# Attention and two expert layers on one core: the first expert product by Strassen's method, fused with the second

## The chip, the core and the metric

The program runs on one core of a Trainium2 chip, whose engines work side by side and wait for each other through semaphores: TensorE (PE; matmuls into PSUM, eight banks of 512 float32 columns by 128 partitions), VectorE (DVE), ScalarE (ACT), GpSimd (POOL) and SyncE (SP), which issues the transfers. The metric is device microseconds of one execution. Three runs of the kernel before took 662.17 to 663.9 us, median 663.18.

## The reference

```python
attn = softmax(mask(q @ k.T / 8)) @ v        # 2 x 8 heads, 576 tokens, 64 wide; local or strided mask
x = attn as (1152, 512)
a = x @ w1;  b = x @ w2                      # (1152, 1024)
x = (a * b @ w3) @ w_out                     # (1152, 512)
p = domain_probs / (domain_probs.sum(-1, keepdims=True) + 1e-09)
for e in range(4):                           # moe2: w1 (4, 512, 1024), w2 (4, 1024, 512)
    h = np.maximum(x @ w1[e], 0.0)
    out += p[:, e:e + 1] * (h @ w2[e])
```

All of it is float32.

## The kernel before

A float32 operand is split into a high part in the reduced format fp32r (a ScalarE cast) and a low part, the rest (a VectorE subtraction). `mm3` (L244) makes a product of two such pairs from three matmuls: high by high, high by low, low by high.

The stages follow each other: attention in 22 tiles; the product a * b (`ab_block`), whose beginning runs beside the attention; w3 @ w_out (`wc_tile`); x3 = ab @ wc (`x3_block`, 16 blocks of 128 features by 288 tokens, 24 matmuls each); then the expert stage, four times over:

- first product (`g1_block`): 8 feature tiles by 3 blocks of 384 tokens. A block is 12 matmuls (4 tiles of 128 inputs, three matmuls each) into one PSUM bank; ScalarE writes relu of it as h_hi (L418), VectorE the rest as h_lo (L419). h for all 1152 tokens stays in SBUF.
- second product (`g2_tile`): 9 tiles of 128 tokens. A tile is 24 matmuls of 512 columns; VectorE scales the result by the token's probability and adds it to the sum (L445, L447). Of the last expert's last tile two halves of 256 columns are made. Finished sums go out at once (L450).

Expert weights come in chunks of 1 MB (`raw_load`), two buffers deep; a chunk is cast and subtracted a piece at a time (`split_hi` L152, `split_lo` L162) by a generator `work()`, which the main loop pushes on by `advance(n)` after each block. A count `live` of the 16 unit buffers (128 x 1024) holds it back. The order of instructions on each engine is that in which this Python code emits them; nothing is reordered. SP issues loads in the order of emission too, each held until its buffer is free.

Of the kernel before, what the change touches and what calls it, by code (L numbers as in the profile page):

```python
# [8 lines left out]
F32 = mybir.dt.float32  # L9
# [31 lines left out]
def kernel(  # L41
# [17 lines left out]
    big = ctx.enter_context(tc.tile_pool(name="big", bufs=16))  # L59
# [5 lines left out]
    small = ctx.enter_context(tc.tile_pool(name="small", bufs=4))  # L65
    ps = ctx.enter_context(tc.tile_pool(name="ps", bufs=5, space=bass.MemoryType.PSUM))
# [41 lines left out]
    class Chunk:  # L108


        def __init__(self, src, wide):
            self.src, self.wide, self.done, self.early = src, wide, False, False

        def raw_load(self):
            if self.wide:
                self.raw = rawp.tile([P, 1024, 2], I32, tag="raw", name="raw64")
                nc.sync.dma_start(out=flat(self.raw), in_=self.src.bitcast(I32))
            else:
                self.raw = rawp.tile([P, 2, 1024], F32, tag="raw", name="raw32")
                nc.sync.dma_start(out=self.raw, in_=self.src.rearrange("c p n -> p c n"))  # L120
# [51 lines left out]
    c_w12 = [Chunk(w12[c], True) for c in range(8)]  # L172
    c_wout = [Chunk(w_out[c], True) for c in range(4)]
    c_w3 = [Chunk(w3T[c], True) for c in range(8)]
    c_e = [Chunk(e12[2 * c:2 * c + 2], False) for c in range(4 * E)]
    live = 8
    stream = c_w12 + c_wout + c_w3 + c_e
    chunk32 = [Chunk(None, False) for _ in range(8 * E)]
# [9 lines left out]
    def work():  # L188


        wide = [c for c in stream if c.wide]
# [30 lines left out]
        for i, c in enumerate(chunk32):  # L222
            pair = c_e[i // 2]
            while live > 14:
                yield False
            c.f32 = pair.raw[:, i % 2]
            c.split_hi()
            yield True
            c.split_lo()
            if i % 2:  # L230
                load_next()
            yield True
# [7 lines left out]
    def need(c):  # L240
        while not c.done:
            assert advance()
# [12 lines left out]
    def load_group(b, g, zeros, cut=0):  # L255


        tq = [big.tile([P, 2, S], F32, tag="big", name="tq") for _ in range(2)]
        tk = big.tile([P, 2, S], F32, tag="big", name="tk")
# [107 lines left out]
    def ab_block(b, ft, n):  # L367
        t = slice(b * S + n * HB, b * S + n * HB + HB)
        if n == 0 and ft % 2 == 0:
            ab_hi[b, ft // 2] = big.tile([P, 2, S], F32R, tag="big", name="ab_hi")  # L370
            ab_lo[b, ft // 2] = big.tile([P, 2, S], F32R, tag="big", name="ab_lo")
# [24 lines left out]
    def x3_block(x3, wc, b, n, ot):  # L396
# [5 lines left out]
        hi, lo = (x[:, ot, t] for x in x3)  # L402
        nc.scalar.copy(hi, acc)
        nc.vector.tensor_tensor(out=lo, in0=acc, in1=hi.bitcast(F32), op=ALU.subtract)


    h_hi, h_lo = {}, {}

    def g1_block(e, x3, ft, n):
        t = slice(n * BLK, n * BLK + BLK)  # L410
        if n == 0:
            h_hi[ft] = big.tile([P, NT], F32R, tag="big", name="h_hi")
            h_lo[ft] = big.tile([P, NT], F32R, tag="big", name="h_lo")
# [4 lines left out]
        nc.scalar.activation(h_hi[ft][:, t], acc, AF.Relu)  # L418
        nc.vector.scalar_tensor_tensor(out=h_lo[ft][:, t], in0=acc, scalar=0.0,  # L419
                                       in1=h_hi[ft][:, t].bitcast(F32), op0=ALU.max, op1=ALU.subtract)  # L420

    pn = const.tile([P, NTT, E], F32, name="pn")
    sums = []
# [9 lines left out]
    def g2_tile(e, tt):  # L433
        t = slice(tt * P, tt * P + P)
        if e == 0 and tt % 2 == 0:
            sums.append(unit("sum", F32))
        total = sums[tt // 2][:, 512 * (tt % 2):512 * (tt % 2) + 512]
        width = 256 if (e, tt) == (E - 1, NTT - 1) else 512
        for c in (slice(c, c + width) for c in range(0, 512, width)):
            acc = bank("g2_acc")[:, c]  # L440
            for k in range(8):
                mm3(acc, (h_hi[k][:, t], h_lo[k][:, t]),
                    chunk32[8 * e + 4 + k // 2].parts(512 * (k % 2) + c.start, width), k == 0, k == 7)
            if e == 0:
                nc.vector.tensor_scalar_mul(total[:, c], acc, pn[:, tt, e:e + 1])  # L445
            else:
                nc.vector.scalar_tensor_tensor(out=total[:, c], in0=acc, scalar=pn[:, tt, e:e + 1],  # L447
                                               in1=total[:, c], op0=ALU.mult, op1=ALU.add)
            if e == E - 1:
                nc.sync.dma_start(out=out[t, c], in_=total[:, c])  # L450

    with tc.manual_schedule():
# [9 lines left out]
        for _ in range(2):  # L462
            pair = big.tile([P, 2, 4, P], F32, tag="big", name="p_pair")
# [55 lines left out]
        wc = [Chunk(None, False) for _ in range(4)]  # L519
# [18 lines left out]
        x3 = (xp.tile([P, 4, NT], F32R, tag="x_hi", name="x3_hi"), xp.tile([P, 4, NT], F32R, tag="x_lo", name="x3_lo"))  # L538
        for b in range(B):
            for i in range(2):  # L540
                for ot in range(4):
                    x3_block(x3, wc, b, i, ot)
                    advance(1)
        for c in wc[:3]:
            c.free()
        live += (NTT + 1) // 2
        for e in range(E):
            for ft in range(8):
                c = chunk32[8 * e + ft // 2]
                need(c)  # L550
                for i in range(NBLK):
                    g1_block(e, x3, ft, i)
                    advance(1)
                if ft % 2:
                    c.free()
            last = chunk32[8 * e + 4:8 * e + 8]
            for c in last:
                need(c)
            for tt in range(NTT):
                g2_tile(e, tt)  # L560
                if tt == NTT - 1:
                    for c in last:
                        c.free()
                advance(2)
# [62 lines left out]
```

## Time and profile before

| | us |
|---|---|
| median of three runs | 663.18 |
| profiled execution, its own time | 663.13 |
| its span, first to last instruction | 661.4 |
| TensorE busy | 647.7 |
| VectorE busy | 305.6 |
| ScalarE busy | 222.5 |

The span is what the engines' records cover; 1.7 us of the execution lie around it. Matmul records overlap, as matmuls are pipelined, so their mean duration is not what one costs; the distance between the ends of equal groups is. The expert stage fills the last 396 us.

### The profile page before, as it was taken

The numbers are of one execution on the slowest core, as the hardware profiler recorded it, in microseconds if no ns is written. First come the engines' busy times: TensorE is split into PE (matmuls) and PEld (weight loads), VectorE is DVE, ScalarE is ACT, GpSimd is POOL, SyncE is SP. The second block draws the span as 40 slices with busy tenths as digits, with TensorE's granted clock in tenths as the row PEclk, the third lists the DMA queues.
The fourth block names the chain that finished last, engine by engine and source line by source line (L and its number), as shares of the span: only waits on it lengthen the run. The fifth ranks groups of instructions, "written<-read, shape, count | busy, mean of one in ns | idle before, by whom it ended". The sixth has DMA issues, their size and how long they took to land.

```text
span 661.4 us, 9113 instructions
## 1 busy us (share of the span) xinstructions
PE 647.7 (98%) x3860; PEld 596.5 (90%) x3860; DVE 305.6 (46%) x514; ACT 222.5 (34%) x502; POOL 6.9 (1%) x18
## 2 busy tenths in 40 slices
PE   8879999999999999999999999999999999999998
PEld 7669989999888999999888999888999888999887
DVE  7999998699775411333212533212533212533111
ACT  5887776466654211223000423000423000422000
POOL 4000000000000000000000000000000000000000
PEclk9989999999999999999999999999999999999999
DMA  8933134154441300011000312000311000300111
GB/s 248 297 108 129 65 128 137 57 172 148 154 165 63 128 1 1 1 65 64 0 1 0 128 64 64 0 1 0 127 64 63 1 1 4 125 1 0 49 48 48
DMA packets 12809, 48.31 MB, mean 73 GB/s; under 512 B 1248, under 2 KB 2528, under 8 KB 10208
## 3 DMA queue, kind: packets, MB, share of 16 engines
q1 hardware_dynamic: 12624, 47.63, 21.9%
q8 instruction: 30, 0.49, 0.3%
q10 hardware_dynamic: 144, 0.10, 0.1%
q14 instruction: 11, 0.09, 0.0%
HBM read 45.37 MB, written 2.36 MB: 72 GB/s over the span
## 4 chain that ended last, share of the span: by engine, by line
PE 91%; DVE 7%; DMA 1%; ACT 0%; issue 0%; SPq 0%
PE g_acc L247 20%; PE g_acc L246 20%; PE g_acc L248 20%; PE ab_acc L246 5%; PE ab_acc L248 5%; PE ab_acc L247 5%; PE x_acc L246 3%; PE x_acc L247 3%; PE x_acc L248 3%; PE wc_acc L248 2%; PE wc_acc L246 2%; PE wc_acc L247 2%; DVE p_pair L326 1%; DVE neg L308 1%; PE sc L302 1%; PE o L345 1%
## 5 line engine op out<-in xcount | busy, mean ns | idle before, releaser
L418 ACT ACTIVATE h_hi<-g_acc 128x384 fp32r<-128x384 f32 x96 | 47.2, 492 | 274.3 <-PE g_acc L248 274.3
L248 PE MATMUL g_acc<-x_hi,w_lo 128*128 128x384 f32 x384 | 128.3, 334 | 0.0
L246 PE MATMUL g_acc<-x_hi,w_hi 128*128 128x384 f32 x384 | 128.3, 334 | 0.0
L247 PE MATMUL g_acc<-x_lo,w_hi 128*128 128x384 f32 x384 | 128.3, 334 | 0.0
L248 PE MATMUL g_acc<-w_hi,h_lo 128*128 128x512 f32 (+1 forms) x296 | 113.5, 384 | 0.0
L247 PE MATMUL g_acc<-w_lo,h_hi 128*128 128x512 f32 (+1 forms) x296 | 113.5, 384 | 0.0
L246 PE MATMUL g_acc<-w_hi,h_hi 128*128 128x512 f32 (+1 forms) x296 | 113.4, 383 | 0.0
L419 DVE SCALAR_TENSOR_TENSOR h_lo<-g_acc,h_hi 128x384 fp32r<-128x384 f32 x96 | 53.5, 558 | 120.2 <-ACT h_hi L418 120.2
L447 DVE SCALAR_TENSOR_TENSOR sum<-g_acc,pn,sum 128x512 f32<-128x512 f32 (+1 forms) x28 | 20.5, 732 | 123.3 <-PE g_acc L248 123.3
L246 PE MATMUL ab_acc<-x_hi,w_hi 128*128 128x288 f32 x256 | 76.5, 299 | 0.0
L248 PE MATMUL ab_acc<-x_hi,w_lo 128*128 128x288 f32 x256 | 75.4, 295 | 0.0
L247 PE MATMUL ab_acc<-x_lo,w_hi 128*128 128x288 f32 x256 | 75.4, 294 | 0.0
L246 PEld LDWEIGHTS g_acc<-x_hi,w_hi 128*128 128x128 f32 x384 | 72.1, 188 | 0.1
L247 PEld LDWEIGHTS g_acc<-x_lo,w_hi 128*128 128x128 f32 x384 | 72.1, 188 | 0.1
L248 PEld LDWEIGHTS g_acc<-x_hi,w_lo 128*128 128x128 f32 x384 | 72.1, 188 | 0.0
L246 PEld LDWEIGHTS g_acc<-w_hi,h_hi 128*128 128x128 f32 x296 | 55.6, 188 | 10.9
L248 PEld LDWEIGHTS g_acc<-w_hi,h_lo 128*128 128x128 f32 x296 | 55.6, 188 | 10.9
L247 PEld LDWEIGHTS g_acc<-w_lo,h_hi 128*128 128x128 f32 x296 | 55.6, 188 | 10.8
L246 PEld LDWEIGHTS ab_acc<-x_hi,w_hi 128*128 128x128 f32 x256 | 48.0, 187 | 1.5 <-issue 0.3
L247 PEld LDWEIGHTS ab_acc<-x_lo,w_hi 128*128 128x128 f32 x256 | 48.0, 188 | 0.0
L248 PEld LDWEIGHTS ab_acc<-x_hi,w_lo 128*128 128x128 f32 x256 | 48.0, 188 | 0.0
L162 DVE TENSOR_TENSOR w_lo<-raw,w_hi 128x1024 fp32r<-128x1024 f32 x32 | 38.8, 1216 | 0.3 <-ACT w_hi L152 0.3
(85 smaller groups left out, 835.8 us busy)
## 6 DMA issues: line engine op xcount, KB each, us to landing
raw<-in_e_dram SPq DMA_DIRECT2D x16, 1024.0 KB, 4.8
raw<-in_w_dram SPq DMA_DIRECT2D x8, 1024.0 KB, 5.0
raw<-in_w3T_dram SPq DMA_DIRECT2D x8, 1024.0 KB, 4.8
raw<-in_w_out_dram SPq DMA_DIRECT2D x4, 1024.0 KB, 4.9
out_dram<-sum SPq DMA_DIRECT2D x8, 256.0 KB, 2.0
tk<-in_kT_dram SPq DMA_DIRECT2D x3, 576.0 KB, 15.8
tq<-in_qT_dram SPq DMA_DIRECT2D x6, 288.0 KB, 13.7
tv<-in_v_loc_dram SPq DMA_DIRECT2D x4, 384.0 KB, 9.9
```

The costliest lines, as they stand in the source:

```text
L162: nc.vector.tensor_tensor(out=self.lo, in0=self.f32, in1=self.hi.bitcast(F32), op=ALU.subtract)
L246: mm(acc, lh, rh, start=first, stop=False)
L247: mm(acc, lh, rl, start=False, stop=False)
L248: mm(acc, ll, rh, start=False, stop=last)
L302: mm(self.sc[:nq, h, :nk], tq[h % 2][:, h // 2, self.q0:self.q0 + nq], tk[:, h // 2, self.k0:self.k0 + nk], start=False, stop=h == 3)
L308: nc.vector.tensor_reduce(out=self.neg[:nq], in_=self.sc[:nq, :, :nk], axis=mybir.AxisListType.X, op=ALU.max, negate=True)
L326: nc.vector.tensor_tensor(out=p, in0=p, in1=rec[:nq].unsqueeze(2).to_broadcast([nq, 4, nk]), op=ALU.mult)
L345: mm(self.o[64 * j:64 * j + 64, k, :nq], vs[k][:nk, self.t, 64 * j:64 * j + 64], self.pT[:nk, 2 * k + j, :nq], start=True, stop=True)
L418: nc.scalar.activation(h_hi[ft][:, t], acc, AF.Relu)
L419: nc.vector.scalar_tensor_tensor(out=h_lo[ft][:, t], in0=acc, scalar=0.0, in1=h_hi[ft][:, t].bitcast(F32), op0=ALU.max, op1=ALU.subtract)
L447: nc.vector.scalar_tensor_tensor(out=total[:, c], in0=acc, scalar=pn[:, tt, e:e + 1], in1=total[:, c], op0=ALU.mult, op1=ALU.add)
```

## The change

Tokens are cut into two halves, of five tiles (640) and four (512), and the whole expert stage runs for the one half and then for the other. A step is one half, one expert and one chunk c of 256 features: 2 x 4 x 4 = 32 steps, 0 to 15 and 16 to 31. In a step the inputs (512) by features (256) matrix of weights and the inputs by tokens matrix are cut in quarters, and h of the step is made of seven products of quarters (`Step.first`) and sums of them; each product has 6 matmuls of 320 or 256 columns. Three PSUM banks a, b, c take the products in turn: a, b, c, a, b, c, a. VectorE adds them into u1, u2, u3, u7 in SBUF (u1 begins as a ScalarE copy), from where ScalarE makes relu (h_hi) and VectorE h_lo. The second product of a step (`Step.second`, 6 matmuls a tile) is interleaved with the first product of the next step: three tiles at the `yield`s of `first`, the others behind it. Its sums stay open in one PSUM bank a tile over the four chunks of an expert, so `g2_acc` holds five banks.

The sums of quarters on the tokens' side are made once for each half (`Tokens.prepare`, eleven pieces): for the first half during the last x3 blocks, for the second in steps 14 and 15. Those on the weights' side are made in the first half (`Weights.work`), written to DRAM as cast pairs, and read back in the second half (`again`); the plain quarters and w2 are loaded and cast twice. x3 is kept as float32.

```diff
-    def g1_block(e, x3, ft, n):
...
-        acc = bank("g1_acc")[:, :BLK]
-        for k in range(4):
-            mm3(acc, chunk32[8 * e + ft // 2].parts(((ft % 2) * 4 + k) * P, P),
-                (x3[0][:, k, t], x3[1][:, k, t]), k == 0, k == 3)
...
+        def work(self):
+            nonlocal live
+            while live > 12:
+                yield False
+            live += 4
+            w = self.raw[:, 0]
...
+            yield from self.split([u[:, :768] for u in plain], w[:, 256:])
...
+            if not self.again:
+                add(a22, a21, a22, ALU.add)
+                add(a21, a11, a21, ALU.subtract)
+                yield True
+                add(a11, a22, a11, ALU.subtract)
+                add(a12, a12, a11, ALU.subtract)
+                yield True
+            sums = [unit("s_hi"), unit("s_lo")]
+            if self.again:
+                for i, u in enumerate(sums):
+                    nc.sync.dma_start(out=u.bitcast(F32), in_=stored[self.at][i])
+            else:
+                yield from self.split(sums, w)
+                for i, u in enumerate(sums):
+                    nc.sync.dma_start(out=stored[self.at][i], in_=u.bitcast(F32))
...
+            self.w2 = [unit("w2_hi"), unit("w2_lo")]
+            yield from self.split(self.w2, self.raw[:, 1])
+            self.done2 = True
+            load_next()
...
+            self.product(a, "a11", "b11")
+            nc.scalar.copy(u1, a)
+            self.product(b, "s2", "t2")
+            self.add(u2, b, u1)
+            work(1)
+            self.product(c, "s3", "t3")
+            self.add(u3, c, u2)
+            work(1)
+            self.product(a, "a12", "b21")
+            self.add(u1, a, u1)
+            self.out(0, 0, u1, 0)
+            yield
+            work(1)
+            self.product(b, "s1", "t1")
+            self.add(u7, b, u3)
+            self.out(1, 1, u7, 0)
+            self.add(u2, b, u2)
+            self.out(0, 0, u1, 1)
+            self.product(c, "a22", "t4")
+            self.add(u3, c, u3)
+            self.out(1, 0, u3, 0)
+            yield
+            self.out(1, 1, u7, 1)
+            work(1)
+            self.product(a, "s4", "b22")
+            self.add(u2, a, u2)
+            self.out(0, 1, u2, 0)
+            self.out(1, 0, u3, 1)
+            yield
+            work(1)
+            self.out(0, 1, u2, 1)
...
+            for i, _ in enumerate(step.first(advance)):
+                tile_of_tokens()
+                if s == 14:
+                    prepare(3, 7)
+            live -= 4
+            for _ in range(3):
+                tile_of_tokens()
```

Where instructions stand now, at three places. First VectorE in an expert's first product. Before, its rows behind those of x3 are the low parts of h (g_acc is the PSUM bank, h_lo the low part), with a low part of weights let in after several blocks:

```order
L404 TENSOR_TENSOR x_lo<-x_acc,x_hi 128x288 x11
L419 SCALAR_TENSOR_TENSOR h_lo<-g_acc,h_hi 128x384 x8
L162 TENSOR_TENSOR w_lo<-raw_2427,w_hi 128x1024
L419 SCALAR_TENSOR_TENSOR h_lo<-g_acc,h_hi 128x384 x6
L162 TENSOR_TENSOR w_lo<-raw_2520,w_hi 128x1024
```

After, one step of the first half, from its second add (m_a, m_b, m_c are the banks; u_3147 is u1, u_3148 u2, u_3149 u3, u_3150 u7; raw_2993 the next step's weights):

```order
L523 TENSOR_TENSOR u_3149<-m_c,u_3148 128x320
L456 TENSOR_TENSOR w_lo<-raw_2993,w_hi 128x768
L523 TENSOR_TENSOR u_3147<-m_a,u_3147 128x320
L470 TENSOR_TENSOR raw_2993<-raw_2993 128x256 x4
L523 TENSOR_TENSOR u_3150<-m_b,u_3149 128x320
L523 TENSOR_TENSOR u_3148<-m_b,u_3148 128x320
L519 SCALAR_TENSOR_TENSOR h_lo<-u_3147,h_hi 128x320
L523 TENSOR_TENSOR u_3149<-m_c,u_3149 128x320
L519 SCALAR_TENSOR_TENSOR h_lo<-u_3150,h_hi 128x320
L456 TENSOR_TENSOR s_lo<-raw_2993,s_hi 128x1024
L523 TENSOR_TENSOR u_3148<-m_a,u_3148 128x320
L519 SCALAR_TENSOR_TENSOR h_lo<-u_3149,h_hi 128x320
```

A dozen operations now belong to one step, where a block had one, and the last read of bank a (u_3148 from m_a) stands behind s_lo.

Second TensorE where the expert stage begins. Before, x3's last block is followed by blocks of the first product, each in a bank of its own:

```order
L246 MATMUL x_acc<-ab_hi,wc_hi 128x288
L247 MATMUL x_acc<-ab_lo,wc_hi 128x288
L248 MATMUL x_acc<-ab_hi,wc_lo 128x288
L246 MATMUL g_acc<-x_hi,w_hi 128x384
L247 MATMUL g_acc<-x_lo,w_hi 128x384
L248 MATMUL g_acc<-x_hi,w_lo 128x384
```

After, the seventh product of step 0 (from b_b_2843) and the first of step 1 (from b_b_2727), both of bank a:

```order
L234 MATMUL m_c<-b_t_2913,w_lo 128x320
L232 MATMUL m_a<-b_b_2843,s_hi 128x320
L233 MATMUL m_a<-b_b_2844,s_hi 128x320
L234 MATMUL m_a<-b_b_2843,s_lo 128x320
L232 MATMUL m_a<-b_b_2727,w_hi 128x320
L233 MATMUL m_a<-b_b_2728,w_hi 128x320
L234 MATMUL m_a<-b_b_2727,w_lo 128x320
```

In step 0 no tile of the second product stands between the two; in every later step two or three do.

Third VectorE in step 14; before, its place is taken by rows like those of the first fence. After (u_4584 is u1 and so on; x_2467 is x3, kept the second half's operands; the L470 row and two L413 rows that only repeat are left out):

```order
L523 TENSOR_TENSOR u_4584<-m_a,u_4584 128x320
L470 TENSOR_TENSOR raw_4482<-raw_4482 128x256 x2
L409 TENSOR_TENSOR kept<-x_2467,kept 128x512 x2
L413 TENSOR_TENSOR x_2467<-x_2467 128x2x256
L523 TENSOR_TENSOR u_4587<-m_b,u_4586 128x320
L523 TENSOR_TENSOR u_4585<-m_b,u_4585 128x320
L519 SCALAR_TENSOR_TENSOR h_lo<-u_4584,h_hi 128x320
L523 TENSOR_TENSOR u_4586<-m_c,u_4586 128x320
L409 TENSOR_TENSOR kept<-x_2467,kept 128x512
L519 SCALAR_TENSOR_TENSOR h_lo<-u_4587,h_hi 128x320
L456 TENSOR_TENSOR s_lo<-raw_4482,s_hi 128x1024
L523 TENSOR_TENSOR u_4585<-m_a,u_4585 128x320
```

Three low parts (L409) and three differences (L413) now stand ahead of the last read of bank a.

## Rows read from the trace of the kernel before

**Rows 1.** The page's busy times and its slices.

```profile
PE 647.7 (98%) x3860; PEld 596.5 (90%) x3860; DVE 305.6 (46%) x514; ACT 222.5 (34%) x502; POOL 6.9 (1%) x18
PE   8879999999999999999999999999999999999998
PEclk9989999999999999999999999999999999999999
```

**Rows 2.** TensorE's waits, the largest: us in total, times, longest.

```profile
PE o L345 <- DVE pT L337: 8.6, 9, 2.0
```

**Rows 3.** Windows: us from:to, length, busy us (count) by engine, clock, DMA share, GB/s.

```profile
165.00:210.00 45.00, 45.00 (x208) 37.70 (x208) 32.24 (x36) 24.68 (x32) 0.00 (x0) 1.00 0.42 140
262.00:312.00 50.00, 50.00 (x290) 50.00 (x289) 16.68 (x27) 14.52 (x27) 0.00 (x0) 1.00 0.12 43
312.00:361.00 49.00, 49.00 (x217) 40.55 (x217) 7.70 (x10) 2.37 (x3) 0.00 (x0) 1.00 0.00 1
361.00:460.00 99.00, 99.00 (x506) 90.55 (x506) 29.21 (x42) 19.30 (x32) 0.00 (x0) 1.00 0.13 43
```

**Rows 4.** Timeline, ScalarE, first expert: start us, us, engine, line.

```profile
264.19 0.49 ACT L418 ACTIVATE h_hi<-g_acc 128x384 fp32r<-128x384 f32 x1 [1.68 <-PE g_acc L248]
266.27 0.49 ACT L418 ACTIVATE h_hi<-g_acc 128x384 fp32r<-128x384 f32 x1 [1.59 <-PE g_acc L248]
```

**Rows 5.** Timeline, VectorE: sums of two tiles, and of the last two half tiles.

```profile
322.96 0.75 DVE L445 TENSOR_SCALAR sum<-g_acc,pn 128x512 f32<-128x512 f32 x1 [3.56 <-PE g_acc L248]
328.40 0.75 DVE L445 TENSOR_SCALAR sum<-g_acc,pn 128x512 f32<-128x512 f32 x1 [4.69 <-PE g_acc L248]
...
655.31 0.48 DVE L447 SCALAR_TENSOR_TENSOR sum<-g_acc,pn,sum 128x256 f32<-128x256 f32 x1 [2.12 <-PE g_acc L248]
658.19 0.48 DVE L447 SCALAR_TENSOR_TENSOR sum<-g_acc,pn,sum 128x256 f32<-128x256 f32 x1 [2.39 <-PE g_acc L248]
```

**Rows 6.** Groups by line and form: busy us, mean ns, idle before.

```profile
L246 PEld LDWEIGHTS g_acc<-x_hi,w_hi 128*128 128x128 f32 x384 | 72.1, 188 | 0.1
L419 DVE SCALAR_TENSOR_TENSOR h_lo<-g_acc,h_hi 128x384 fp32r<-128x384 f32 x96 | 53.5, 558 | 120.2 <-ACT h_hi L418 120.2
L162 DVE TENSOR_TENSOR w_lo<-raw,w_hi 128x1024 fp32r<-128x1024 f32 x32 | 38.8, 1216 | 0.3 <-ACT w_hi L152 0.3
L152 ACT CAST w_hi<-raw 128x1024 fp32r<-128x1024 f32 x32 | 32.9, 1042 | 0.0
L381 DVE TENSOR_TENSOR ab<-ab_acc,ab 128x288 f32<-128x288 f32 x32 | 14.4, 452 | 4.4 <-PE ab_acc L248 4.4
L383 ACT CAST ab_hi<-ab 128x288 fp32r<-128x288 f32 x32 | 14.0, 438 | 8.7 <-DVE ab L381 8.5
L379 ACT COPY ab<-ab_acc 128x288 f32<-128x288 f32 x32 | 12.9, 404 | 4.0 <-PE ab_acc L248 3.9
L159 DVE TENSOR_TENSOR wc_lo<-wc_raw,wc_hi 128x512 fp32r<-128x512 f32 x2 | 1.4, 692 | 5.6 <-ACT wc_hi L158 5.6
L362 DVE TENSOR_TENSOR x_lo<-o,x_hi 128x216 fp32r<-128x216 f32 x6 | 3.3, 552 | 0.0
```

**Rows 7.** Timeline, VectorE: two independent neighbours.

```profile
62.91 0.45 DVE L385 TENSOR_TENSOR ab_lo<-ab,ab_hi 128x288 fp32r<-128x288 f32 x1
63.28 0.45 DVE L381 TENSOR_TENSOR ab<-ab_acc,ab 128x288 f32<-128x288 f32 x1
```

**Rows 8.** Timeline: the end of an x3 block, and its readers.

```profile
245.95 0.29 PE L246 MATMUL x_acc<-ab_hi,w_hi 128*128 128x288 f32 x1
246.15 0.40 ACT L403 CAST x_hi<-x_acc 128x288 fp32r<-128x288 f32 x1 [2.76 <-PE x_acc L248]
246.58 0.46 DVE L404 TENSOR_TENSOR x_lo<-x_acc,x_hi 128x288 fp32r<-128x288 f32 x1 [2.70 <-ACT x_hi L403]
```

**Rows 9.** Transfers by issuing line: count, KB each, median us to landing.

```profile
raw<-in_e_dram SPq DMA_DIRECT2D x16, 1024.0 KB, 4.8
out_dram<-sum SPq DMA_DIRECT2D x8, 256.0 KB, 2.0
```

More of the change, by code (lines that the diff above doesn't have):

```diff
@@ L65 @@
     small = ctx.enter_context(tc.tile_pool(name="small", bufs=4))
+    big = [tc.tile_pool(name=f"big{b}", bufs=8, side=side).__enter__() for b, side in enumerate(("right", "left"))]
     ps = ctx.enter_context(tc.tile_pool(name="ps", bufs=5, space=bass.MemoryType.PSUM))
@@ L221, in work @@
         yield True
[L222 to L232, printed above, removed]
+        for w in c_e:
+            yield from w.work()
     worker = work()
@@ L238, in advance, with need @@
         return all([next(worker, False) for _ in range(n)])
-    def need(c):
-        while not c.done:
+    def need(c, part=0):
+        while not (c.done if part == 0 else c.done1 if part == 1 else c.done2):
             assert advance()
@@ L431, in load_probs @@
         nc.vector.tensor_tensor(out=pn, in0=pn, in1=den.unsqueeze(2).to_broadcast([P, NTT, E]), op=ALU.mult)
[L433 to L450, printed above, removed]
+    c_e = [Weights(again, e, c) for again in range(2) for e in range(E) for c in range(4)]
+    stream += c_e
     with tc.manual_schedule():
@@ L518 @@
         raw = xp.tile([P, 8, 512], F32, tag="x_hi", name="wc_raw")
[L519 removed]
+        wc = [Chunk(None) for _ in range(4)]
         for c in c_wout:
@@ L537 @@
             advance(5)
[L538 to L543, printed above, removed]
+        c = None
+        x3 = xp.tile([P, 4, NT], F32, tag="x_lo", name="x3")
+        halves = [Tokens(0, 5, lambda name, i, n: ops.tile([P, 2, 320], F32R, tag="op", name=f"b_{name}{i}")),
+                  Tokens(5, 4, lambda name, i, n: keep(name, i, n))]
@@ new lines, with keep @@
+        keeps = iter(range(9))
+        def keep(name, i, n):
+            k = next(keeps, None)
+            if k is not None:
+                return kept[:, k]
+            return ops.tile([P, 2, 320], F32R, tag="op", name=f"b_{name}{i}")[:, :, :n]
+        for b, i in ((0, 0), (0, 1), (1, 0), (1, 1)):
+            if (b, i) == (1, 0):
+                big[0].release()
+                ops = ctx.enter_context(tc.tile_pool(name="ops", bufs=14, side="right"))
+                early = halves[0].prepare(x3)
+            for ot in range(4):
+                x3_block(x3, wc, b, i, ot)
+                advance(1)
+                if (b, i) == (1, 0) and ot < 2:
+                    next(early)
+                elif (b, i) == (1, 1):
+                    for _ in range(4):
+                        next(early, None)
@@ L544 @@
         for c in wc[:3]:
             c.free()
[L546 to L552, printed above, removed]
-                    advance(1)
[L554 to L564, printed above, removed]
+        big[1].release()
@@ new lines, with prepare @@
+        hp = ctx.enter_context(tc.tile_pool(name="hp", bufs=6))
+        scr = ctx.enter_context(tc.tile_pool(name="scr", bufs=4))
+        kept = xp.tile([P, 9, 2, 256], F32R, tag="x_hi", name="kept")
+        live += 3
+        steps = [Step(half, e, c, c_e[16 * i + 4 * e + c])
+                 for i, half in enumerate(halves) for e in range(E) for c in range(4)]
+        later = halves[1].prepare(x3)
+        prepared = 0
+        def prepare(n, limit):
+            nonlocal prepared
+            for _ in range(n):
+                if prepared < limit:
+                    prepared += 1
+                    next(later, None)
@@ new lines, with tile_of_tokens @@
+        for s, step in enumerate(steps):
+            need(step.w, 1)
+            before = steps[s - 1] if s else None
+            todo = iter(range(len(before.half.tts)) if s else ())
+            if s:
+                need(before.w, 2)
+            def tile_of_tokens():
+                i = next(todo, None)
+                if i is not None:
+                    before.second(i)
+                    advance(1)
+                    if s == 15:
+                        prepare(3, 99)
+            for i, _ in enumerate(step.first(advance)):
[5 more added lines that the diff above has]
+                tile_of_tokens()
+            if s:
+                live -= 2
+            if s == 16:
+                live -= 1
@@ L568, in _layouts @@
+        for i in range(len(step.half.tts)):
+            step.second(i)
 def _layouts(x):
```

163 lines of the change are left out of this document (130 added, 33 removed).

## The prediction

> **What bounds the kernel now.** I read the page's busy times and slices first [rows 1]: TensorE is busy for 647.7 of 661.4 us, in nine tenths of a slice or more from the fourth to the last but one, and the granted clock stands at its upper level, 2.4 GHz, in every slice but the third. TensorE's waits come next: of the three that the view lists the largest is 8.6 us, for the transposed probabilities of the attention [rows 2]; the others belong to the warm-up and the attention's first load, so none falls in the expert stage that the change rewrites. The windows [rows 3] show that stage: TensorE fills 50 of 50, 49 of 49 and 99 of 99 us, while VectorE works 16.7, 7.7 and 29.2 of them, and the DMA engines are busy for 0.13 at most. So the expert stage costs what its matmuls cost, and VectorE has room.
>
> What a matmul costs is the spacing of groups, not the duration of a row, since the durations overlap. A block of the first product (12 matmuls of 384 columns) ends every 2.08 us [rows 4], 173.3 ns each; a token tile of the second (24 of 512) every 5.44 us, 226.7 ns each; the last half tile (24 of 256) takes 2.88 us, 120.0 ns each [rows 5]. All three are columns/2.4 GHz plus 13.3 ns, also across the ends of groups of 12 and of 24, so a group's start costs nothing by itself. An expert is 24 x 2.08 + 9 x 5.44 = 98.88 us, four are 395.5, and the split last tile adds 2 x 2.88 - 5.44 = 0.3: 395.8 us. The trace agrees: from 264.19 - 2.08 to 658.19 are 396.1.
>
> **What the change removes and adds on TensorE.** Seven quarter products stand where eight did. In the first half (five token tiles) a product is 6 matmuls of 320 columns, by the law above 133.3 + 13.3 = 146.7 ns each, so 0.88 us, and seven are 6.16; a tile's two pieces of the second product are 6 x 226.7 ns = 1.36 us, five are 6.80. A step takes 12.96 us. In the second half a product is 6 x 120.0 = 0.72, seven 5.04, four tiles 5.44: 10.48. Sixteen of each are 207.4 + 167.7 = 375.0, with 4 x 0.08 for the split last tile 375.4. The removal is 395.8 - 375.4 = **20.5 us**, all of it in the first product (199.7 to 179.2; an eighth of its columns would be 23.0, and 192 more matmuls at 13.3 ns give back 2.6). Lower bound of the rest is zero: TensorE cannot run these matmuls closer than its own spacing.
>
> [...] The rows first: a weight load lasts 188 ns [rows 6], longer than the 120.0 ns from one 256-column matmul to the next [rows 5], so loads and matmuls run beside each other here. [...]
>
> **VectorE, in a step of the first half.** Durations: an add at 320 elements 485 ns (452 at 288, and 1.04 ns an element between 288 and 1024), at 256 elements 419, a low part at 768 950 and at 1024 1216, a low part of h 492 (558 at 384); on ScalarE the copy from PSUM 430, a relu 465, the casts 830 and 1042 [rows 6]. Independent neighbours overlap by 0.08 us [rows 7]. A reader starts 0.20 us after the next group's first matmul, and VectorE 0.03 after ScalarE [rows 8]. A step holds seven adds 3.4, four low parts of h 2.0, the weights' 768 and twice 1024 3.4, four sums of weights 1.7: 10.5 us of 12.96. That fits, but the order is strict, so I lay one step out, t = 0 at its first matmul. The products end at 0.88, 1.76, 2.64, 3.52, then a tile, 5.76, 6.64, a tile, 8.88, and three tiles until 12.96. VectorE: u2 from 1.96, u3 from 2.84, the 768 until 4.2, u1 until 4.6, the weights' sums until 6.35, u7 6.75, u2 7.15, low part 7.55, u3 8.0, low part 8.4. The next, s_lo, waits for ScalarE's s_hi (relu of u3 until 8.5, cast until 9.45): 9.5 to 10.7. Then u2's last add, which frees bank a, ends at 11.1; two low parts 12.1; w2_lo, behind its cast, 12.6 to 13.8, while the next step's first add is due at 14.9. The next step's first product needs bank a at 12.96: 1.9 us of cover. Where an expert ends, five sums of output (0.75 each, [rows 5]) are let in, and the add ends at 12.3, the step's rest at 16.2; the next step starts its adds 1.25 us late and frees the bank at 12.3 again. Cover 0.7, cost nothing. The second half has neither sums nor s_lo: about 7 us of 10.48.
>
> **Three places where it does not fit.** (1) Step 0 has no tiles behind its seventh product: the next step's first product wants bank a at 6.16, and VectorE, with the 1.2 us of w2_lo between, ends that add at 7.45. **1.3 us**. (2) Steps 14 and 15 also prepare the second half's operands. Step 14 takes seven more operations of 512 elements on VectorE (692 ns, [rows 6]) and four casts on ScalarE, about 0.62 each by the same kind of slope. Six of the seven and the wait for one cast behind s_hi come ahead of the add: the weights' sums are pushed to 8.6, u7 9.0, the third low part waits for its cast until 12.4, s_lo ends at 15.2, the add at 15.6, where bank a was wanted at 12.96: **2.6 us**. Step 15 starts its adds at 3.2 and ends the add at 12.7: nothing. (3) The tail: after the last matmul a half tile's sum and its transfer stay as they were, but the transfers ahead of it follow at 1.36 us rather than 5.44; at 2.0 us from issue to landing [rows 9] I take **0.2**.
>
> Hidden at no cost: the preparation of the first half (eleven operations, about 8 us, beside the last five x3 blocks of 0.40 + 2.76 = 3.16 us, [rows 8]; by the same layout the last ends 1.0 us ahead of step 0; uncovered it would cost that 8). The first sums of weights stand in front of the first x3 copies on ScalarE, about 2 us late, against five banks of 3.2 us.
>
> **Transfers.** Each step of the first half now stores 1 MB and loads 1 MB, each of the second loads 2 MB. A 1 MB load lands in 4.8 us; a 256 KB store in 2.0, so 1 MB of stores lies between 2 and 8 us [rows 9]: 12.8 at most of 12.96, and nothing waits for a store until two steps on. Two loads in line are 9.6 of 10.48 us; the window with the most transfers moved 140 GB/s at 0.42 of the engines' time [rows 3], which is 333 at full time, so 2 MB (2.1 million bytes) would take 6.3. Each has a step or more of lead. SP's queue carries them in order, raw, s_hi, s_lo; a load waits there for w2_lo or for a bank of weights that TensorE has left, and only the step after next is behind it. I take zero; both ends stay below.
>
> **The sum.** The profiled execution took 663.13 us (661.4 of span and 1.7 around it), the median of the three runs is 663.18, so the one stands for the other. 663.13 - 20.5 + 1.3 + 2.6 + 0.2 = **646.8 us**.
>
> **Rivals.**
> - No wait at all (642.7 to 645): the layout's latencies are too long. For it: I let each read wait 0.20 us. Against: place (1) is a chain without slack.
> - Small waits in every step (650 to 657): at 0.2 to 0.6 us in each of 16 steps of the first half, 3 to 10 us. For it: the cover at the ends of experts is 0.7 us, less than my errors in 17 durations added up. Against: 1.9 in the other steps.
> - VectorE becomes the bound of the first half, and the kernel slower: the gain of 16.4 is gone when a step takes 1.0 us longer, so when the chain to bank a ends at 14.0, not 11.1: every operation of the 9.1 us from its first add a third dearer. At 40% the add ends 1.8 us late in each of 16 steps: 675. For it: a copy-out of 216 elements took 552 ns in the strided form against 452 for 288 in a row [rows 6]. Against: all new operands are runs of 256 or more elements.
> - The second half's loads become the bound: a step would need 11.5 us for 2 MB, 182 GB/s. At the 140 of the busiest window they take 15.0: 646.8 + 16 x 4.5 = 719. Against: that window's engines were idle for more than half.
> - Weight loads in the open: 192 x 188 ns = 36 us: 683. Against: the 120.0 ns above. [...]
>
> **How the numbers follow.** The forecast (its own range 645 to 650) 0.68, no wait 0.08, small waits 0.15, VectorE the bound 0.05, loads the bound 0.02, weight loads 0.01, something unseen 0.01. The range must leave out no more than 0.2: from the end that TensorE's spacing sets, 643, to the top of the small waits, 657. Faster or slower counts from 0.3%, 2 us, about what a measurement of this kernel tells from no change: the first three cases are all faster, and VectorE just past its bound could land on either side: faster 0.91, same 0.03, slower 0.06.
>
> **What would show it.** In the profile after, TensorE's groups of the first product 0.88 and 0.72 us apart, tiles 1.36; the stage from first product to last matmul near 379 us; TensorE's waits on VectorE (the add that frees bank a) once after the seventh product of step 0 and once after step 14, 1 to 3 us each, and few others; VectorE about 10 us busy in a step of the first half. It is wrong if TensorE waits on the same add or on s_lo in most steps, if a wait on a DMA of s_hi or raw shows in the second half, or if the spacing at 320 columns is not near 147 ns.

## The result and the profile after

| | before | after | ratio (95%) |
|---|---|---|---|
| time, median, us | 663.17 (662.17 to 663.90, 4 runs) | 648.09 (646.75 to 648.42, 4 runs) | 0.977 (0.9751 to 0.9789) |
| profiled execution, us | 663.13 | 648.42 (span 646.6) | |
| expert stage, start of its first to start of its last matmul, us | 261.91 to 657.87 | 262.25 to 643.14 | |

646.8 us was forecast. The page's busy times and slices, which answer to [rows 1]:

```profile
PE 629.1 (97%) x4052; PEld 572.7 (89%) x4052; DVE 470.6 (73%) x888; ACT 291.7 (45%) x628; POOL 6.9 (1%) x18
PE   7769999999999999999999999999999999999998
PEclk9989999999999999999999999999999999999999
```

TensorE is still what fills the span, at a granted clock of 0.9 or more of full speed in every slice but the third, as before. VectorE has gone from 46% to 73%. TensorE's waits, all six that the view lists (us in total, times, longest), against [rows 2]:

```profile
PE o L331 <- DVE pT L323: 8.6, 9, 2.0
PE sc L288 <- DMA tq<-in_qT_dram: 2.6, 4, 1.0
PE idle L106 <- DVE idle L101: 1.1, 1, 1.1
PE m_a L232 <- ACT u L533: 0.9, 1, 0.9
PE m_b L234 <- DVE s_lo L456: 0.5, 1, 0.5
PE m_b L234 <- DMA s_lo<-stored: 0.4, 1, 0.4
```

The last three lines are new. Only they lie in the expert stage: 1.8 us. None is for bank a behind u2's last add, which was the wait forecast at places 1 and 2. Five windows (us from:to, length, busy us and count by engine, clock, DMA share, GB/s), against [rows 3]: an ordinary step of the first half; a step's length in which an expert's sums of output fall; step 17, the step of the second half with the load wait; the time from the issue of that load to the matmul that waited for it; and a step's length with sums of output in the second half:

```profile
334.02:347.14 13.12, 13.12 (x74) 11.78 (x73) 10.24 (x19) 4.98 (x9) 0.00 (x0) 1.00 0.49 173
420.10:433.20 13.10, 13.10 (x73) 11.77 (x72) 12.47 (x24) 4.93 (x8) 0.00 (x0) 1.00 0.44 159
479.13:490.31 11.18, 10.79 (x67) 9.56 (x66) 7.92 (x15) 4.44 (x8) 0.00 (x0) 1.00 0.87 310
473.33:480.63 7.30, 6.91 (x38) 5.75 (x36) 5.33 (x11) 2.31 (x5) 0.00 (x0) 1.00 0.90 329
512.20:522.70 10.50, 10.50 (x69) 9.47 (x68) 8.56 (x17) 3.72 (x7) 0.00 (x0) 1.00 0.38 132
```

A step of the first half takes 13.12 us and one of the second 10.51 (forecast 12.96 and 10.48). VectorE works 10.2 of 13.1 (forecast 10.5), and 12.5 where sums of output fall. The groups that answer to [rows 6] (busy us, mean ns, idle before):

```profile
L456 DVE TENSOR_TENSOR w_lo<-raw,w_hi 128x768 fp32r<-128x768 f32 x32 | 30.4, 950 | 5.0 <-ACT w_hi L454 5.0
L519 DVE SCALAR_TENSOR_TENSOR h_lo<-u,h_hi 128x320 fp32r<-128x320 f32 x64 | 31.0, 484 | 1.7
L523 DVE TENSOR_TENSOR u<-m_b,u 128x320 f32<-128x320 f32 x48 | 21.9, 485 | 14.6 <-PE m_b L234 14.6
L523 DVE TENSOR_TENSOR u<-m_b,u 128x256 f32<-128x256 f32 x48 | 18.9, 421 | 39.8 <-PE m_b L234 39.8
L233 PEld LDWEIGHTS m_b<-b_t,s_hi 128*128 128x128 f32 x128 | 24.1, 188 | 1.3
```

The adds at 320 and 256 elements take the 485 and 421 ns that were laid out (485, 419), the low part 484 (492), the 768 950. The weight loads still take 188 ns, while 256-column matmuls start 118.4 ns apart (mean of the 420 in steps 18 to 27): loads and matmuls run side by side.

### The profile page after: what moved, and what is told of

It reads as the page before. It is cut to its first block, busy times and chain, and to the rows that moved or that the text cites. A ratio compares the mean times of both kernels' runs of the same rounds, so it can differ in the third digit from the quotient of the medians.

```text
span 646.6 us, 10360 instructions
## 1 busy us (share of the span) xinstructions
PE 629.1 (97%) x4052; PEld 572.7 (89%) x4052; DVE 470.6 (73%) x888; ACT 291.7 (45%) x628; POOL 6.9 (1%) x18
## 4 chain that ended last, share of the span: by engine, by line
PE 85%; DVE 8%; DMA 3%; ACT 2%; SPq 1%; issue 1%; DVEq 0%
PE g_acc L233 10%; PE g_acc L234 10%; PE g_acc L232 10%; PE ab_acc L232 5%; PE ab_acc L234 4%; PE ab_acc L233 4%; PE m_a L232 4%; PE m_a L234 4%; PE m_a L233 4%; PE x_acc L232 3%; PE x_acc L233 3%; PE x_acc L234 3%; PE m_b L234 3%; PE m_c L232 3%; PE m_c L233 3%; PE m_c L234 3%
## 5 line engine op out<-in xcount | busy, mean ns | idle before, releaser
L517 ACT ACTIVATE h_hi<-u 128x320 fp32r<-128x320 f32 (+1 forms) x128 | 56.9, 445 | 189.2 <-DVE u L523 189.2
L523 DVE TENSOR_TENSOR u<-m_b,u 128x320 f32<-128x320 f32 (+1 forms) x96 | 40.8, 453 | 54.4 <-PE m_b L234 54.4
L456 DVE TENSOR_TENSOR w_lo<-raw,w_hi 128x768 fp32r<-128x768 f32 x64 | 69.4, 1085 | 12.0 <-ACT w_hi L454 11.9
L519 DVE SCALAR_TENSOR_TENSOR h_lo<-u,h_hi 128x320 fp32r<-128x320 f32 (+1 forms) x128 | 57.7, 451 | 3.5 <-ACT h_hi L517 1.4
L454 ACT CAST w_hi<-raw 128x768 fp32r<-128x768 f32 x64 | 59.9, 936 | 0.0
L303 ACT ACTIVATE p_pair<-sc,neg 96x128 f32<-96x128 f32 (+3 forms) x88 | 30.4, 355 | 18.5 <-DVE neg L296 17.3
L233 PE MATMUL m_b<-b_t,s_hi 128*128 128x320 f32 (+1 forms) x128 | 37.8, 295 | 0.0
L523 DVE TENSOR_TENSOR u<-m_a,u 128x320 f32<-128x320 f32 (+1 forms) x64 | 28.9, 452 | 11.8 <-PE m_a L234 11.8
L456 DVE TENSOR_TENSOR s_lo<-raw,s_hi 128x1024 fp32r<-128x1024 f32 x16 | 19.6, 1225 | 23.2 <-ACT s_hi L454 23.2
L121 ACT ACTIVATE raw<-raw 128x1024 int32<-128x1024 uint32 x20 | 23.5, 1174 | 27.4 <-DMA raw<-in_w3T_dram 19.5
```

The source lines that it names most:

```text
L121: nc.scalar.activation(self.low, self.low.bitcast(U32), AF.Copy, scale=2.0 ** -29)
L233: mm(acc, lh, rl, start=False, stop=False)
L303: nc.scalar.activation(self.p[:nq, h, :nk], self.sc[:nq, h, :nk], AF.Exp, bias=self.neg[:nq, h:h + 1], scale=SCALE, accum_out=self.sum[:nq ...
L454: nc.scalar.copy(dst[0], src)
L456: nc.vector.tensor_tensor(out=dst[1], in0=src, in1=dst[0].bitcast(F32), op=ALU.subtract)
L517: nc.scalar.activation(hi, src, AF.Relu)
```

## The experiments

### Place 2: where step 15 loses 2 us

```profile
453.92 0.41 PE L234 MATMUL m_b<-b_t,s_lo 128*128 128x320 f32 x1 [0.49 <-DVE s_lo L456]
456.60 0.41 PE L232 MATMUL m_a<-b_b,w_hi 128*128 128x320 f32 x1 [0.95 <-ACT u L533]
```

These are TensorE's two waits in step 15 (timeline; in brackets the idle time before and its releaser). VectorE and ScalarE at that time:

```profile
451.63 0.69 DVE L413 TENSOR_TENSOR x<-x 128x512 f32<-128x512 f32 x1
452.65 1.22 DVE L456 TENSOR_TENSOR s_lo<-raw,s_hi 128x1024 fp32r<-128x1024 f32 x1
```

```profile
454.68 0.60 ACT L408 CAST kept<-x 128x512 fp32r<-128x512 f32 x1
455.19 1.04 ACT L454 CAST w_hi<-raw 128x1024 fp32r<-128x1024 f32 x1
456.13 0.42 ACT L533 COPY u<-m_a 128x320 f32<-128x320 f32 x1
```

The second product needs s_lo, which VectorE began at 452.65, behind the moved-in preparation of 451.63. The fourth product needs bank a, and ScalarE's copy of it (456.13) stood behind two casts, one of them preparation (454.68). So the preparation is late, as forecast, but it is met in two other places than the bank. Test: spread it.

```diff
-                if s == 14:
-                    prepare(3, 7)
+                if 8 <= s <= 14 and i == 0:
+                    prepare(1, 7)
```

> The first seven pieces of the preparation of the second half's tokens are spread, one per step, over steps 8 to 14, in place of seven in step 14. Theory (the 2 us that step 15 is longer than its neighbours, 15.10 against 13.12, come from those pieces: VectorE and ScalarE are late with s_lo and with the copy of u1): step 15 shrinks to about 13.1, 646.1 in all. Rival 1 (step 15 waits for what every last step of an expert or of a half has to wait for): step 15 keeps 15.1, 648.1. Rival 2 (one extra piece per step pushes VectorE over its cover, since only 0.7 us are spare at an expert's end): steps 8 to 14 grow by tenths each, 648 to 650.

645.92 us, ratio to before 0.9751 (0.9737 to 0.9764). All of TensorE's waits that are left, and step 15:

```profile
PE o L331 <- DVE pT L323: 10.1, 10, 2.0
PE sc L288 <- DMA tq<-in_qT_dram: 1.9, 3, 0.9
PE idle L106 <- DVE idle L101: 1.1, 1, 1.1
```

```profile
451.33:464.45 13.12, 13.12 (x73) 11.78 (x72) 9.35 (x17) 5.68 (x11) 0.00 (x0) 1.00 0.49 175
```

Step 15 takes 13.12 us, with TensorE busy in all of it. The preparation was the cause, and rivals 1 and 2 fall: steps 8 to 14 stay at 13.12. Step 17 falls from 11.18 to 10.52 as well: its load wait is not there in this run.

### Place 1: why there is no wait

After the change, the end of step 0 and the start of step 1 (TensorE), and u2's last add (VectorE):

```profile
268.26 0.31 PE L234 MATMUL m_a<-b_b,s_lo 128*128 128x320 f32 x1
268.41 0.31 PE L232 MATMUL m_a<-b_b,w_hi 128*128 128x320 f32 x1
...
270.17 0.31 PE L232 MATMUL m_c<-b_t,s_hi 128*128 128x320 f32 x1
```

```profile
269.03 0.48 DVE L523 TENSOR_TENSOR u<-m_a,u 128x320 f32<-128x320 f32 x1
```

The add ends at 269.51, 7.26 us into the step (laid out: 7.45). But step 1's first product starts at 268.41 without waiting. The section on the change calls both products "of bank a"; that is their name, not their bank. In the compiled program the three banks of step 0 are 7, 6, 5 for a, b, c, and those of step 1 are 6, 5, 7: the pool hands out the bank that was freed first. The old bank a is the next step's c, wanted at 270.17 only. Test: allocate the banks once.

```diff
-            a, b, c = (ps_sc.tile([P, 512], F32, tag="sc", name=f"m_{i}")[:, :n] for i in "abc")
+            if not banks:
+                banks.extend(ps_sc.tile([P, 512], F32, tag="sc", name=f"m_{i}") for i in "abc")
+            a, b, c = (m[:, :n] for m in banks)
```

> Banks a, b, c of the seven products are allocated once, so that every step writes its first product into the same bank. Theory (the wait foreseen at place 1 is missing because the pool gives each step's first product the bank that was freed first, which is the old b, two VectorE operations earlier): with fixed banks the wait comes back, about 1.1 us at the start of step 1 (the last read of bank a ended 269.52, the step began 268.41), about 2.2 us at the start of step 15 (454.27 against 452.1), and some tenths at every step whose start now falls ahead of the last read of the old a; 1 to 6 us in all, 649 to 654. Rival (VectorE is simply earlier than I laid it out, the rotation does nothing): no wait on bank a, 648.1 as before.

650.46 us, ratio 0.9818 (0.9805 to 0.9831). The same place, and the sum of such waits:

```profile
268.55 0.31 PE L234 MATMUL m_a<-b_b,s_lo 128*128 128x320 f32 x1
269.85 0.41 PE L232 MATMUL m_a<-b_b,w_hi 128*128 128x320 f32 x1 [0.99 <-DVE u L523]
```

```profile
269.31 0.48 DVE L523 TENSOR_TENSOR u<-m_a,u 128x320 f32<-128x320 f32 x1
```

```profile
PE m_a L232 <- DVE u L523: 3.1, 2, 2.1
```

Step 0 grows from 6.16 to 7.31 us and step 1 by 0.12: 1.27, where 1.3 was forecast. Steps 14 and 15 come to 3.9 us above 13.12 in sum (after the change 2.0). Step 14 takes 15.43: the add that the preparation pushes back now holds up bank a, TensorE waits for it for 2.1 us, and the step grows by 2.3, where place 2 forecast 2.6. Step 15 takes 14.75, and TensorE is busy in all of it; but after that wait the granted clock stood at 0.50 for 3.4 us, and 320-column matmuls started 0.27 us apart in place of 0.15. Step 15, and that stretch of it:

```profile
456.04:470.79 14.75, 14.75 (x73) 13.40 (x74) 10.98 (x21) 7.24 (x13) 0.00 (x0) 0.88 0.47 179
457.50:460.92 3.42, 3.42 (x15) 3.42 (x14) 2.98 (x6) 1.42 (x3) 0.00 (x0) 0.50 0.19 38
```

The other steps stay at 13.13, so the "tenths at every step" of the expectation did not come. The layout of VectorE was right; what it lacked is the order in which the pool hands out banks.

### Where the gain comes from

Eight plain products in the same frame (halves, fusion and interleaving kept; no sums of quarters, nothing stored or loaded):

```diff
-            self.product(a, "a11", "b11")
...
-            self.out(0, 1, u2, 1)
+            self.quarter(0, 0)
+            work(2)
+            self.quarter(1, 0)
...
+            self.quarter(0, 1)
...
+            self.quarter(1, 1)
```

> The changed kernel with eight plain products of quarters in place of Strassen's seven: relu reads PSUM directly, no sums of quarters are made, stored or loaded; halves, fusion and interleaving stay. Theory (the gain is TensorE's columns alone): 16 steps longer by six matmuls of 320 columns (0.88 us) and 16 by six of 256 (0.71), 25.4 us, less the 2 to 3 us of waits that VectorE's sums brought: about 671 (669 to 674). Rival (the gain comes from the fusion pair by pair and from open banks, not from Strassen): 648 to 655.

671.32 us, ratio 1.0134 (1.012 to 1.0148). The theory holds, 671 forecast. Halves and fusion without Strassen cost about 8.7 us against before; the seventh of eight products gives 23.2 back. Of the 8.7, about 5 are by estimate the 384 more matmuls of the first product at 13.3 ns (what the spacings of [rows 4] and [rows 5] hold besides the columns), and 3.6 are the spacing dealt with below.

### How much VectorE may still take on

```diff
             self.out(0, 1, u2, 1)
+            for _ in range(1):
+                nc.vector.tensor_tensor(out=junk, in0=junk, in1=junk, op=ALU.subtract)
```

> The changed kernel with one useless VectorE operation (128x1024, 1.22 us by the steps' own 128x1024 differences) at the end of the sums of each of the 32 steps. Theory (VectorE's cover is 1.9 us in an ordinary step, 0.7 at an expert's end): hidden in ordinary steps; 0.5 to 0.6 us more in each of the first half's expert ends and some tenths more around step 15, 1 to 4 us in all, 649 to 652. Rival (the sums are already on the path, TensorE waits for them in every step): 1.2 us in each of 31 steps, 686.

> The same with three such operations (3.66 us) per step. Theory: beyond the cover by 1.76 us in each of 15 steps of the first half (26 us) and more at the expert ends; in the second half VectorE's 6.0 us become 9.7 of 10.5 (hidden), 8.6 become 12.3 at four or eight steps (1.8 each, 7 to 14): 680 to 695. Rival (VectorE works in gaps that the layout did not see, cover 3 us or more): 648 to 658.

With one: 648.71 us, ratio 0.9779 (0.9762 to 0.9795), 0.6 us more than without it and just below the 649 to 652 expected. Steps 1 to 14 stay at 13.12, those with sums of output too, so the 0.5 to 0.6 us expected at each expert's end did not come: the cover there is at least 1.2 us, where 0.7 was laid out. Only steps 15 and 16 grow (by 1.0 and 0.3). With three: 687.35 us, ratio 1.0364 (1.0347 to 1.038), 39 us more. An ordinary step there, 14.50 us long (VectorE, then TensorE, then its wait in sum):

```profile
284.97 3.73 DVE L564 TENSOR_TENSOR junk<-junk 128x1024 f32<-128x1024 f32 x3
288.62 1.22 DVE L456 TENSOR_TENSOR w_lo<-raw,w_hi 128x1024 fp32r<-128x1024 f32 x1
289.76 0.48 DVE L523 TENSOR_TENSOR u<-m_b,u 128x320 f32<-128x320 f32 x1
```

```profile
290.29 0.41 PE L232 MATMUL m_b<-b_t,s_hi 128*128 128x320 f32 x1 [1.10 <-DVE u L523]
```

```profile
PE m_b L232 <- DVE u L523: 20.2, 15, 3.5
```

14.50 is 1.38 more than 13.12, so 2.28 of the 3.66 us were covered; 1.9 was laid out. The wait that decides is not the next step's bank a, but the fifth product's bank b, behind the late u2. Where sums of output fall, the steps take 18.3 to 19.4. There the wait is 3.5 us, and within it or shortly after it the granted clock falls to 0.50; the first such stretch:

```profile
334.85:341.68 6.83, 5.49 (x17) 5.02 (x18) 6.62 (x14) 1.28 (x3) 0.00 (x0) 0.50 0.47 155
```

With step 15's, four such stretches are 23.9 us long. An estimate from the matmuls started in them, set against their spacing at a granted clock of 1.00, gives about 9 of the profiled execution's 40 us (688.09 against 648.42) to the clock, which over the whole execution was 0.978, after the change 0.997. After the waits of 1.10 us of the ordinary steps it stayed at 1.00. So the rival "VectorE becomes the bound" is real: in an ordinary step it begins at about 2.3 us more work (at an expert's end between 1.2 and 3.66), and at 3.66 it has taken the whole gain and 24 us more.

### Why a 512-column matmul takes 232 ns

The distances between starts in the trace give 231.8 ns on average for the 840 matmuls of the second product (before 226.9), 4.1 us in all. An example from a row of 18 (two matmuls, six starts apart):

```profile
304.98 0.39 PE L232 MATMUL g_acc<-w_hi,h_hi 128*128 128x512 f32 x1
...
306.38 0.39 PE L232 MATMUL g_acc<-w_hi,h_hi 128*128 128x512 f32 x1
```

1.40 us for six, 233 each, and it stays so to the end of the row: 228, 237, 229, 238, 229, 237 and on. Before, the first nine after a change of width took 224 to 236, and all behind them 226.7. Three causes were thought of. First, the open banks, six matmuls each in turn, put into the kernel before:

```diff
-    def g2_tile(e, tt):
...
+    def g2_group(e, tts):
+        accs = {}
+        for q in range(4):
+            for tt in tts:
...
+                    for k in (2 * q, 2 * q + 1):
+                        mm3(acc, (h_hi[k][:, t], h_lo[k][:, t]),
+                            chunk32[8 * e + 4 + k // 2].parts(512 * (k % 2) + c.start, width), k == 0, k == 7)
```

> The kernel before, with the second product of an expert made in pieces of six matmuls that go round five (then four) open banks, as the changed kernel does it, with nothing between the pieces. Theory A (512-column matmuls take 231 to 233 ns instead of 226.7 because their accumulations alternate between open banks six at a time): 232 ns, 864 matmuls by 5 ns, 4.5 us longer, 667 to 668. Theory B (the spacing comes from the narrower layout of the hidden values or from the switches between streams of 320 or 256 and of 512 columns): 226.7 ns, 663.

662.48 us, ratio 1.0002 (0.9993 to 1.0011). Six starts take 1.36 us:

```profile
330.44 0.39 PE L246 MATMUL g_acc<-w_hi,h_hi 128*128 128x512 f32 x1
...
331.80 0.39 PE L246 MATMUL g_acc<-w_hi,h_hi 128*128 128x512 f32 x1
```

That is 226.7 ns: not the banks. Second, the rows' length:

```diff
             for i, _ in enumerate(step.first(advance)):
-                tile_of_tokens()
+                advance(1)
...
-            for _ in range(3):
+            for _ in range(5):
                 tile_of_tokens()
```

> The changed kernel with all tiles of the second product behind the seventh product, in place of three between the products: 30 (second half 24) matmuls of 512 columns in a row in place of 6, 6 and 18 (12). Theory A (a matmul's 226.7 ns are a settled state, which the ten matmuls after each change of width fall short of): the first ten of each row stay at 229 to 238, the others fall to 226.7, about 2.5 us less, 645.5. Theory B (where hidden values and weights lie in SBUF against one another sets the spacing): 231 to 233 to the end of each row, 648 as before, or more if sums now come late for a bank.

651.14 us, ratio 0.9816 (0.9801 to 0.9831). Twelve starts from the middle of a row of 30:

```profile
304.09 0.39 PE L232 MATMUL g_acc<-w_hi,h_hi 128*128 128x512 f32 x1
...
306.89 0.39 PE L232 MATMUL g_acc<-w_hi,h_hi 128*128 128x512 f32 x1
```

2.80 us, 233 each, to the end of the row: theory A falls. It is even 3 us slower: with nothing between the products, VectorE's sums come late where an expert ends (three such steps take 13.62 to 13.65, 1.5 us in all), and step 15 takes 15.70 (0.6 more); the rest is spread over the other steps and was not followed up. Third, addresses. In the compiled program the second product's moving weights start at 96 modulo 512 bytes in SBUF in both kernels; its stationary tiles (hidden values) at 96 before and at 480 after. Two edits that move nothing but addresses, one in each kernel:

```diff
+        pad = ctx.enter_context(tc.tile_pool(name="pad", bufs=1))
+        pad.tile([P, 32], F32, name="pad")
         hp = ctx.enter_context(tc.tile_pool(name="hp", bufs=6))
```

> The changed kernel with 128 unused bytes ahead of the pool of the hidden values, so that the stationary tiles of the second product start at the same address modulo 512 bytes as the moving weights (96 and 96, as in the kernel before) in place of 384 bytes apart (480 and 96). Theory B (addresses): 512 columns back at 226.7 to 228 ns, 840 matmuls by 4 to 5 ns, 3.4 to 4.3 us less, 643.8 to 644.7. Theory A (switches of width, the order of the work): unchanged, 648.1 and 231.8 ns.

```diff
     big = ctx.enter_context(tc.tile_pool(name="big", bufs=16))
+    pad = ctx.enter_context(tc.tile_pool(name="pad", bufs=1))
+    pad.tile([P, 32], F32, name="pad")
     xp = ctx.enter_context(tc.tile_pool(name="xp", bufs=1))
```

> The kernel before with 128 unused bytes between the pool that holds the hidden values and all pools behind it: only the second product's stationary tiles come to lie 128 bytes off its moving weights modulo 512 (96 and 224); its order stays. Theory B (addresses): 512 columns at 231 to 233 ns, 840 by 4 to 5 ns, 666 to 667. Theory A (order): 226.9 ns, 662.6.

The kernel before with the pad: 667.82 us, ratio 1.0066 (1.005 to 1.0083), with a tile's sums 5.57 us apart, where they were 5.44 [rows 5]:

```profile
323.32 0.75 DVE L447 TENSOR_SCALAR sum<-g_acc,pn 128x512 f32<-128x512 f32 x1 [3.70 <-PE g_acc L250]
328.89 0.75 DVE L447 TENSOR_SCALAR sum<-g_acc,pn 128x512 f32<-128x512 f32 x1 [4.82 <-PE g_acc L250]
```

That is 232 ns each, and it never settles over rows of 216. The changed kernel with the pad: 646.20 us, ratio 0.9741 (0.9722 to 0.9759). Six starts in a row of 18, 1.36 us:

```profile
304.62 0.39 PE L232 MATMUL g_acc<-w_hi,h_hi 128*128 128x512 f32 x1
...
305.98 0.39 PE L232 MATMUL g_acc<-w_hi,h_hi 128*128 128x512 f32 x1
```

Theory B holds: addresses decide here whether the spacing settles, at 226.7 ns, or stays near 232. But the gain is half of the 3.4 to 4.3 expected: steps of 13.05 and 10.47 us, 0.07 and 0.04 less. The reason is in the rows: after each change of width the first five matmuls still take 228 to 236, and 12 of a step's 30 stand in groups of six that never get further (mean 230.8; rows of 18: 228.0). Besides, the 320-column matmuls went from 146.3 to 147.0 ns, which gives back 0.03 us a step. So both theories had a half of it. Two more distances:

```diff
-        pad.tile([P, 32], F32, name="pad")
+        pad.tile([P, 64], F32, name="pad")
```

> As the run with 128 unused bytes ahead of the hidden values, but 256: stationary tiles of the second product at 224 modulo 512, moving weights at 96, so 128 bytes apart (the changed kernel: 384; the kernel before: 0). If only equal addresses modulo 512 settle, the spacing is about 231.8 ns and the steps 13.12 and 10.51 us; if every distance but 384 settles, 229 to 230 ns in the groups of six and 226.7 at the end of the rows of 18, steps 13.05 and 10.47 us.

The same line with 96:

> The same with 384 bytes: stationary tiles at 352, moving weights at 96, 256 bytes apart. If what counts is the address modulo 256, the spacing settles to 226.7 ns in the rows of 18 as with 128 bytes (steps 13.05 and 10.47 us); if modulo 512, it does not (231 to 233 ns, 13.12 and 10.51 us).

One run each, 647.68 and 645.28 us, so the spacing in the trace decides here, not the time. Six starts, 128 bytes apart and then 256 bytes apart:

```profile
304.92 0.39 PE L232 MATMUL g_acc<-w_hi,h_hi 128*128 128x512 f32 x1
...
306.32 0.39 PE L232 MATMUL g_acc<-w_hi,h_hi 128*128 128x512 f32 x1
```

```profile
304.38 0.39 PE L232 MATMUL g_acc<-w_hi,h_hi 128*128 128x512 f32 x1
...
305.74 0.39 PE L232 MATMUL g_acc<-w_hi,h_hi 128*128 128x512 f32 x1
```

1.40 and 1.36 us: steps of 13.12 and 10.51 in the first, 13.05 and 10.47 in the second. So with distances of 0 and 256 the spacing settled (1.36 us for six), with 128 and 384 it did not (1.40).

### Both repairs together

The edits of the spread preparation and of the 128 bytes:

> Both the spread preparation and the 128 bytes ahead of the hidden values. Theory B: the two add up, 645.9 less 3.4 to 4.3, 641.6 to 642.5. Theory A: 645.9.

644.34 us, ratio 0.9715 (0.97 to 0.973): 0.0055 below the change's 0.977, 3.6 us. Theory B's 641.6 to 642.5 took the pad at 3.4 to 4.3 us; beside the spread preparation alone (645.92) it gives 1.6.

## Why the prediction was right, and where it was off

The time was 1.3 us above the forecast by medians. The terms, in the profiled execution (648.42, 1.6 above):

| term | forecast | measured | by |
|---|---|---|---|
| TensorE's columns, matmuls counted at 226.7, 173.3, 146.7, 120.0 ns | -20.5 | 395.7 to 375.3: -20.5 (counted, not timed) | counts in both traces; eight products cost 23.2 more in all |
| place 1, bank a at step 1 | +1.3 | 0 | 1.27 with fixed banks |
| place 2, preparation | +2.6 | +2.0 | gone when spread |
| place 3, tail | +0.2 | 0 | last start to end of span 3.5 us in both |
| a load of s_lo, step 17 | 0 | +0.7 | wait of 0.4; two starts 0.67 and 0.22 us apart in place of 0.12 each |
| spacing off the law | 0 | +2.8 | 512 columns +4.1, 320 -0.3, 256 -1.0 |
| start of the stage | 0 | +0.3 | 262.25 against 261.91 |

-20.5 + 2.0 + 0.7 + 2.8 + 0.3 is -14.7: 663.13 to 648.4. That the sum is only 1.6 off is in part luck: 3.8 us that no term foresaw (spacing, load, start) stand against 2.1 us of waits and tail that came smaller or not at all.

- The bound and the main term were right: TensorE's columns decide, and VectorE's sums are hidden.
- Place 1: the failing step is "the next step's first product wants bank a". The chain to the add was laid out to 0.2 us, but I took letters for banks. The order of the pool put 1.76 us (two products) between.
- Place 2: 2.0 where 2.6 was forecast is near by luck, since the route was wrong by the same step. The preparation did push the last reader of bank a (it ended 15.3 us into step 14, laid out at 15.6), and with fixed banks TensorE waits for it; with the rotating ones nothing wants that bank then. What TensorE met were s_lo and u1's copy in step 15, a step that the layout put at nothing. With fixed banks the place cost 3.9, as the granted clock stood at 0.50 for 3.4 us after the wait; the layout had no term for that.
- "All three are columns/2.4 GHz plus 13.3 ns, also across the ends of groups": this was read from rows of 216 equal matmuls. The 2.4 GHz is the slope of the spacings of [rows 4] and [rows 5], (226.7 - 120.0) ns over 256 columns or 0.417 ns each, not a reading of the clock, which the profile gives only as a share of full speed. The transition was in the trace of before (the first nine after a change of width), and I did not look at it, nor at where the new tiles would lie. It was the largest miss, partly balanced by place 1 and by 256 columns at 118.4 ns.
- Transfers: the stage's loads were taken as hidden; in step 17 one came 0.4 us late. The failing step is "each has a step or more of lead": this load was issued at 473.33, 6.7 us ahead of the matmul that wants it, not the 10.5 and more of a step, and in that time the DMA engines were busy for 0.90 and moved 329 GB/s (fourth row of the windows above). With the preparation spread, with fixed banks, and with 128 and 256 bytes of padding that wait is not there; with 384 bytes and with both repairs it is 0.2, so it sits at the edge.
- Rivals: no wait at all (642.7 to 645) is what the spread preparation made, at 645.9, with 2.8 of spacing in it; small waits in every step are not there, since no wait is listed in steps 1 to 13, and the 0.16 us by which these steps exceed 12.96 are spacing; VectorE is not the bound, by the margin measured above; loads as bound and weight loads in the open are shown false by steps of 10.5 us at 118.4 ns.

## What to carry over

When a layout by hand says that a bank is wanted, follow the bank and not the name: a rotating pool changes who meets whom, and work pushed into a step can show at another consumer than the one laid out. When a rewrite replaces long rows of equal matmuls by short ones with new tiles, read the spacing behind a change of width in the old trace and compare the start addresses of stationary and moving tiles in both programs; 128 bytes of padding were worth 1.6 to 1.9 us here. A kernel whose spare engine is filled to 78% of a step has a margin to be measured: one 1.22 us operation per step cost 0.6 us in all, three cost more than the whole gain. And a wait of TensorE's can cost more than itself: with one of 2.1 us, and with those of 3.5, the granted clock fell to 0.50, for 3.4 us after the one and for 6.8 at the first of the others.

## What was not expected of the hardware

- 512-column float32r matmuls, each with its own weight load, settled at 226.7 ns where stationary and moving tiles started 0 and 256 bytes apart in SBUF modulo 512, and stayed in a pattern of 228 to 241 ns, mean 232, where they started 128 and 384 bytes apart. 0 and 384 were seen in both kernels, 128 and 256 in the changed one, with one run each. Why is open: no view shows it. Other distances were not tried. At 320 columns the tiles are 128 bytes off too, and took 146.4 ns, where 146.7 was laid out. At 256 columns the same offset did no harm: in the kernel before, the last half tiles took 118.7 ns with the pad and 119.8 without it.
- Settling took five to nine matmuls after a change of width: 0.02 to 0.04 us each time (0.02 behind 320 or 256 columns with the pad, 0.04 behind 384 in the kernel before).
- Fixing banks a, b, c alone changed the pattern of the first half's 512-column rows from 228/237 in turn to a cycle of six from 228 to 241 (mean 232.5 to 231.3), and the 320-column ones from 146.3 to about 147.3, though every SBUF address stayed. Why is open; it was not followed up.
- The granted clock fell inside a busy stage: with fixed banks it stood at 0.50 from 457.50 to 460.92, 1.5 us after a wait of 2.1 us, and 320-column matmuls took 0.27 us each there. In the changed kernel itself the waits of 0.49 and 0.95 us in step 15 left it at 1.00.
